# Scores and values of a gated linear attention by halves of keys, without the square above the diagonal

## The chip, the cores and the metric

The kernel runs on one core of a Trainium2 chip. The metric is the device time of one execution in microseconds (us). The kernel before took 387.55 us, the median of three runs (387.32 to 389.53).

A core has five engines that run their own instruction streams and wait for each other through semaphores: TensorE (PE in the profile, with its weight loads apart as PEld), VectorE (DVE), ScalarE (ACT), GpSimd (POOL) and SyncE (SP, which here issues most transfers). TensorE multiplies a stationary operand, loaded first, with a moving operand, and writes its result to PSUM. Its array can be split by rows and columns into tiles that work side by side; a matmul's `tile_position` names its tile.

## The reference

Four batches, eight heads, 768 tokens, 48 values a head: a recurrent state, then a two-layer block with a softmax-like unit and a norm.

```python
for t in range(S):
    state = alpha[:, :, t, :, None] * state + np.einsum('bhd,bhe->bhde', k[:, :, t], v[:, :, t])
    y[:, :, t] = np.einsum('bhd,bhde->bhe', q[:, :, t], state)
x = y.transpose(0, 2, 1, 3).reshape(B * S, H * D)      # 3072 x 384
h = x @ w_in                                           # 384 x 1024
sm = softmax(h); solu = h * sm
ln = (solu - mean(solu)) / np.sqrt(var(solu) + 1e-06) * g_ln
out = ln @ w_out                                       # 1024 x 384
```

Everything is float32.

## The kernel before, in words

**Groups.** The 768 tokens are cut into six groups of 128 (`G`), each for all four batches. For one group the attention part is done for all batches and heads at once. The 48 values of a head are split into 32 "firsts" and 16 "lasts", and the lasts of two heads share one block of 32. So q and k lie as (batch, 32 values) on the 128 partitions, token in the free dimension: `kT[quarter(b), block]`, `qv[quarter(b), block]`. Scans on VectorE (`scan_back`, `scan_on`) make the decays within a group, and q and k are multiplied with them, so that a plain product of q and k has the decay in it.

**Attention of a group**, in the order of its steps:

- `scores(g, half)`: four heads of all four batches. For each head two matmuls of 32 rows of contraction (firsts, then lasts) give a square of 128 keys on the partitions by 128 queries in the free dimension. The four batches use the four row tiles. Each batch has a PSUM bank of its own (`a0` to `a3`).
- `masked(half)`: VectorE multiplies each bank with an upper triangular mask of 128 columns (a query reads keys up to itself) and writes `sT` in SBUF; one operation of 512 columns a bank.
- `read_begin`, `read_state(half)`: from group 1 on, the old state times q, into PSUM banks `y` (they are the same four banks). Here the contraction is 64 rows, two batches at once, and the output is split in four column tiles: eight tiles.
- `read_values(g)`: 16 pieces (`parts`) of 32 output columns a batch, with the 128 keys as rows: `vn` (the values, token on the partitions, each head in 64 columns) is stationary, `sT` moves. Four column tiles. It goes batch by batch, and ScalarE copies each batch's bank to `x` when that batch is done.
- `next_state(g)`: products of `kg` (k with token on the partitions) and `vn` in two banks `kv`, which are `a0` and `a1` again, and an add to the state on VectorE.

**The block after it.** For each group `up` makes `h` in eight steps of 512 columns (L390), ScalarE the exp (L404), VectorE h times exp (L405), ScalarE its square (L406), and POOL and VectorE running sums (`running`, L421). `down` (L501) multiplies with `w_out`, in two halves for each of the group's four batches; `finish` scales and stores.

**What sets the order.** It is written by hand: each engine executes its instructions in program order. From group 1 on a loop runs over steps 0 to 7 of `up` of group g. In each step stand `up`, half a `down` of the group before it, and what a table names for the attention of group g+1: in the table `usual` `"v keys"` at step 0, the lasts and firsts of q at 2, `scores0` at the end of step 4, `masked0` at the head of 5, `scores1` at the end of 5, `masked1` at the head of 6, `read0` at 6, `read1` in 7, and `values` (with `next_state`) at the end of 7. In `first`, for the attention of group 2, there is no `down` yet. The attention of groups 0 and 1 is written out before the loop, with the unpacking of the weights: `fetch` brings them as 64-bit values into `room`, `bits` turns them to float32 on VectorE, and `in_range` tests their exponents on ScalarE, with a buffer `sq` in between.

**Queues.** `load_v(g)` puts four transfers on SP's queue. Behind it on the same queue come the loads of k, the moves of q to the rows of the state (`move_lasts`, `move_firsts`), the loads of q and alpha, and the stores of the output.

Of the kernel before, what the change touches and what calls it, by code (L numbers as in the profile page):

```python
# [32 lines left out]
def fast_path(ctx, tc, q, k, v, alpha, moe_w_in, moe_w_out, moe_g_ln, out):  # L33
# [12 lines left out]
    nc = tc.nc  # L46
    B, H, S, D = q.shape
    NTOK, DM = out.shape
# [3 lines left out]
    NP = H // 2  # L52
    NB = H + NP
    E0, E1 = 32, 16
    KC = DM // P
# [9 lines left out]
    const = pool("const", 1)  # L65
    ring = pool("ring", 3)
    work = pool("work", 2)
# [7 lines left out]
    ctx.enter_context(tc.manual_schedule())  # L75

    ident = const.tile([P, P], FP, name="ident")
    mask = const.tile([P, P], FP, name="mask")
    ones = const.tile([P, P], FP, name="ones")
    small_ones = const.tile([P, 32], FP, name="small_ones")  # L80
    parity = const.tile([P, 2], FP, name="parity")
# [23 lines left out]
    HW = 64  # L105
    VW = H * HW + E1
    vn = const.tile([P, B, VW], FP, name="vn")
    state = const.tile([P, 2, VW], FP, name="state")
    SW = P + 1
    lot = const.tile([P, 4 * 768], FP, name="lot")  # L110
# [58 lines left out]
    def held(x, n):  # L169

        return x[:, n, 0 : H * HW].rearrange("p (h e) -> p h e", e=HW)[:, :, E1:HW]

    def load_v(g):
        t = slice(g * P, (g + 1) * P)
        for b in range(B):
            nc.sync.dma_start(out=held(vn, b), in_=v[b, :, t, :].rearrange("h p d -> p h d"))

    def firsts(src, dst):
        nc.vector.transpose(out=dst.rearrange("p h (t u) -> p h u t", u=TQ), in_=src[:, :, :, 0:E0])  # L179
# [11 lines left out]

    def alpha_over(g):
        x = an.rearrange("p h u d -> p (h u d)")
        sq = one.tile([P, 768], FP, name="sq").bitcast(U8)[:, 0 : x.shape[1]]
# [73 lines left out]
    def quarter(b):  # L268
        return slice(32 * b, 32 * b + 32)

    def banks(name, shape, n=B):
        return [ps_a.tile([P] + shape, FP, tag=f"a{b}", name=f"{name}{b}") for b in range(n)]

    def scores(g, half, a=None):
        a = a or banks("a", [NP, P])
        for i in range(NP):
            h = half * NP + i
            for kb, qb in ((h, h), (H + h // 2, H + h)):
                for b in range(B):
                    nc.tensor.matmul(  # L280
                        a[b][:, i], lhsT=kT[quarter(b), kb], rhs=qv[quarter(b), qb, 0:P], start=kb == h, stop=kb != h,
                        tile_position=(32 * b, 0), skip_group_check=True,
                    )
        masks[half] = a

    masks = {}

    def masked(half, batches=range(B)):
        a = masks[half]
        for b in batches:  # L290
            nc.vector.tensor_tensor(  # L291
                out=sT[:, b, half * NP : half * NP + NP], in0=a[b], in1=mask[:, None, :].to_broadcast([P, NP, P]),
                op=ALU.mult,
            )

    def keys_back(g, t=None):
        t = t or banks("tp", [NP, P], 3)
# [25 lines left out]
    parts += [(3 * j + 1, 2 * j + 1, last) for j in range(NP)]  # L323
    reading = {}

    def y_mm(b, n, row, lhsT, rhs, stop=False):
        begun = reading["begun"]
        a, r = divmod(n, 4)
        nc.tensor.matmul(  # L329
            y_bank(b)[quarter(r), a], lhsT=lhsT, rhs=rhs, start=(b, r) not in begun, stop=stop,  # L330
            tile_position=(row, 32 * r), skip_group_check=True,
        )
        begun.add((b, r))
# [5 lines left out]
    def y_bank(b):  # L339
        if b not in reading["y"]:  # L340
            reading["y"][b] = ps_a.tile([P, KC, P], FP, tag=f"a{b}", name=f"y{b}")
        return reading["y"][b]
# [9 lines left out]
    def read_values(g, batches=range(B)):  # L352
        if 0 in batches:
            gr[g]["x"] = pair.tile([P, KC, B, P], FP, name="x")
# [93 lines left out]
    def token_sums(g):  # L448


        d = gr[g]
        t = ps_a.tile([P, B, 2, 32], FP, tag="a3", name="rows") if g else ps_h.tile([P, B, 2, 32], FP, tag="h", name="rows")
        for b in range(B):
            for r in range(4):
                c = b * P + 32 * r
                nc.tensor.matmul(
                    t[quarter(r), b], lhsT=d["unit"][:, 0:32], rhs=d["p"][:, :, c : c + 32], start=True, stop=True,
                    tile_position=(0, 32 * r), skip_group_check=True,
                )
        tt = work.tile([P, B, 2, 32], FP, name="cols")  # L460
# [45 lines left out]
    def finish(n):  # L506
        g, b = divmod(n, B)
        d = st[n]
        s, o = sums[:, n], d["o"][:, 0:DM]
        t0 = b * S + g * P  # L510
        if g == G - 1:
            o_sb = work.tile([P, DM], FP, name="o_sb")
            r = gr[g]["r"][:, b : b + 1]
            nc.vector.tensor_scalar(out=o_sb[:, 0:P], in0=o[:, 0:P], scalar1=r, scalar2=None, op0=ALU.mult)  # L514
            nc.scalar.activation(out=o_sb[:, P:DM], in_=o[:, P:DM], func=AF.Copy, scale=r)  # L515
            nc.scalar.dma_start(out=out[t0 : t0 + P, :], in_=o_sb)
            d.clear()
            return
        nc.vector.tensor_copy(out=s[:, 0:1], in_=d["o"][:, DM : DM + 1])
        t = small.tile([P, 1], FP, name="t")  # L520
        nc.vector.scalar_tensor_tensor(
            out=t, in0=s[:, 0:1], scalar=-1.0 / DFF, in1=s[:, 0:1], op0=ALU.mult, op1=ALU.mult
        )
        nc.vector.tensor_tensor(out=s[:, 3:4], in0=t, in1=gr[g]["s"][:, b : b + 1], op=ALU.add)  # L524
        if g == 0:

            o = work.tile([P, DM], FP, name="o_mean")
# [91 lines left out]
    def mean(half):  # L619


        m = ps_h.tile([P, 512], FP, tag="h", name="sums")[:, 0:DM]
        if half == 0:
            for f in range(FC):
                r = quarter(f % 4)
                nc.tensor.matmul(
                    m[r], lhsT=ones[:, 0:32], rhs=w_out[:, f, 0:DM], start=f < 4, stop=f >= FC - 4,
                    tile_position=(0, r.start), skip_group_check=True,
                )
            made["m"] = work.tile([P, DM], FP, name="o_mean")  # L630
# [14 lines left out]
    nc.scalar.dma_start(out=mask, in_=inline(np.triu(np.ones((P, P))), "mask_c"))  # L645
# [764 lines left out]
```

## Time and profile before

| | |
|---|---|
| median of three runs | 387.55 us |
| the profiled execution: time, span | 388.88 us, 387.1 us |
| TensorE busy, records | 365.6 us (94%), 4341 matmuls and 4341 weight loads |
| VectorE, ScalarE, GpSimd busy | 250.7, 144.5, 111.5 us |
| `h` (L390), `o` (L501) on PE | 134.8, 133.1 us |
| scores in banks `a` (L280) on PE | 26.2 us, 704 records |
| values, and reads of the state (L329), on PE | 22.6 us, 768 records; 11.9 us, 640 records |
| mask (L291) on VectorE | 27.3 us, 44 of 683 ns, and 4 in other banks |
| copies of `x` (L359) on ScalarE | 11.2 us, 24 of 480 ns |
| mean granted TensorE clock | 0.989 |

The span is the time from the first to the last instruction of one profiled execution. A float32 matmul leaves two matmul records and two weight-load records. The busy time of a line counts overlapping records once, so 704 records of 289 ns make 26.2 us, since four tiles work side by side. "Idle before" is how long the engine stood still just ahead of a group of instructions, with what ended it. "issue" is a stall that ended with nothing that the profile shows as released. "PEclk" is the share of TensorE's full clock that was granted.

### The profile page before, as it was taken

To read this page: it belongs to the slowest core of one execution; us is meant where nothing else is said; L and a number is where in the kernel's file an instruction comes from. 1 tells how busy PE (TensorE), PEld (TensorE's weight loads), DVE (VectorE), ACT (ScalarE), POOL (GpSimd) and SP (SyncE) were. 2 spreads that over 40 slices of the span, in tenths; PEclk is the share of its full clock that TensorE was granted. 3 is DMA by queue.
4 is the path that set the end of the run, shared out by engine and by line. 5 is a ranking of instruction groups with operands and counts; after the bars stand their busy time and mean duration, and the time that the engine had idled before them with its cause. 6 is when DMAs were issued, how large, how long until landed. Compare 5 with 4: busy or idle time off the path is not lost. (4 is left out here: it accounts for less than half of the span.)

```text
span 387.1 us, 10060 instructions
## 1 busy us (share of the span) xinstructions
PE 365.6 (94%) x4341; PEld 219.3 (57%) x4341; DVE 250.7 (65%) x413; ACT 144.5 (37%) x255; POOL 111.5 (29%) x122
## 2 busy tenths in 40 slices
PE   8798899988979998999999999998999999999994
PEld 8685335656645556555557555665556565555652
DVE  0989878996997858885584875664875413444600
ACT  2628566681415426134253153342142132222100
POOL 6000000000232992437130466210475211323200
PEclk9989999999989999999999999999999999999999
DMA  9891978248355535717142627003123000000011
GB/s 182 166 323 51 221 220 200 47 97 183 92 131 104 116 79 102 147 35 161 37 105 47 140 62 172 13 11 70 36 63 89 22 16 8 23 21 20 22 44 47
DMA packets 72439, 36.05 MB, mean 93 GB/s; under 512 B 48185, under 2 KB 69953, under 8 KB 72385
## 3 DMA queue, kind: packets, MB, share of 16 engines
q1 hardware_dynamic: 71360, 34.39, 37.6%
q10 hardware_dynamic: 1024, 0.92, 0.7%
q8 instruction: 36, 0.59, 0.7%
q14 instruction: 19, 0.15, 0.1%
HBM read 25.30 MB, written 4.72 MB: 78 GB/s over the span
## 5 line engine op out<-in xcount | busy, mean ns | idle before, releaser
L390 PE MATMUL h<-x,w_in 128*128 128x512 f32 x288 | 134.8, 608 | 3.4 <-DVE room L405 1.6
L501 PE MATMUL o<-w_out,room 128*128 128x385 f32 x384 | 133.1, 491 | 1.1 <-DVE least L218 1.1
L501 PEld LDWEIGHTS o<-w_out,room 128*128 128x128 f32 x384 | 71.6, 190 | 56.8 <-issue 15.3
L390 PEld LDWEIGHTS h<-x,w_in 128*128 128x128 f32 x288 | 53.1, 192 | 63.5 <-issue 49.2
L405 DVE TENSOR_TENSOR room<-h,e 128x512 f32<-128x512 f32 x40 | 27.7, 693 | 62.6 <-ACT e L404 62.6
L404 ACT ACTIVATE e<-h 128x512 f32<-128x512 f32 x40 | 23.9, 597 | 89.1 <-PE h L390 88.5
L421 POOL TENSOR_TENSOR p<-p,e 128x512 f32<-128x512 f32 x30 | 40.8, 1360 | 21.9 <-ACT e L404 21.5
L406 ACT ACTIVATE u<-room 128x512 f32<-128x512 f32 x40 | 25.2, 630 | 42.5 <-DVE room L405 42.5
L532 POOL TENSOR_TENSOR r<-sums,mhalf 128x1 f32<-128x1 f32 x20 | 12.5, 626 | 91.5 <-DVE sums L524 91.5
L291 DVE TENSOR_TENSOR sT<-a,mask 128x512 f32<-128x512 f32 x44 | 27.3, 683 | 15.3 <-PE a L280 15.3
L280 PE MATMUL a<-qv,kT 32*128 32x128 f32 x704 | 26.2, 289 | 3.9 <-DVE least L218 2.0
L280 PEld LDWEIGHTS a<-qv,kT 32*128 32x128 f32 x704 | 23.2, 196 | 11.0 <-issue 2.3
L421 DVE TENSOR_TENSOR p<-p,u 128x512 f32<-128x512 f32 x30 | 23.6, 786 | 8.4 <-ACT u L406 8.4
L204 DVE TENSOR_TENSOR_SCAN hT<-aT,unit 128x516 f32<-128x516 f32 x18 | 22.3, 1285 | 8.7 <-ACT aT L677 8.6
L204 DVE TENSOR_TENSOR_SCAN aT<-aT,seed 128x516 f32<-128x516 f32 x18 | 25.0, 1391 | 0.6
L329 PE MATMUL y<-sT,vn 128*32 128x128 f32 x768 | 22.6, 273 | 0.4 <-DVE sT L291 0.4
L329 PEld LDWEIGHTS y<-sT,vn 128*32 128x32 f32 x768 | 20.7, 110 | 2.9 <-issue 2.0
L228 POOL TENSOR_TENSOR kT<-kT,hT 128x1024 f32<-128x1024 f32 (+1 forms) x8 | 13.3, 1682 | 29.8 <-DVE kT L179 29.8
L359 ACT COPY x<-y 128x384 f32<-128x384 f32 x24 | 11.2, 480 | 22.7 <-PE y L329 22.7
L196 ACT ACTIVATE sq<-an,mone 128x1536 uint8<-128x1536 f32 x12 | 18.9, 1572 | 0.2
L243 POOL COPY qe<-hT 128x4 f32<-128x4 f32 x5 | 1.0, 191 | 59.4 <-DVE hT L204 59.4
L534 ACT ACTIVATE o_sb<-o,r 128x384 f32<-128x384 f32 x16 | 9.3, 581 | 17.2 <-POOL r L532 17.2
(142 smaller groups left out, 370.2 us busy)
## 6 DMA issues: line engine op xcount, KB each, us to landing
vn<-in_v_dram SPq DMA_DIRECT2D x24, 192.0 KB, 4.5
an<-in_alpha_dram SPq DMA_DIRECT2D x20, 192.0 KB, 4.1
out_dram<-o_sb SPq DMA_DIRECT2D x20, 192.0 KB, 2.0
room<-in_moe_w_in_dram SPq DMA_DIRECT2D x6, 512.0 KB, 7.5
room<-in_moe_w_out_dram SPq DMA_DIRECT2D x8, 384.0 KB, 4.3
kn<-in_k_dram SPq DMA_DIRECT2D x16, 192.0 KB, 3.9
qn<-in_q_dram SPq DMA_DIRECT2D x16, 192.0 KB, 4.7
lot<-qe SPq DMA_DIRECT2D x40, 64.5 KB, 2.1
```

The costliest lines, as they stand in the source:

```text
L196: nc.scalar.activation(out=sq, in_=x, func=AF.Relu, scale=sign, bias=mone, accum_out=over[:, g, i : i + 1])
L204: nc.vector.tensor_tensor_scan(out=o, data0=a, data1=s, initial=1.0, op0=ALU.mult, op1=ALU.add)
L228: nc.gpsimd.tensor_tensor(out=kT[:, part], in0=kT[:, part], in1=hk[:, part], op=ALU.mult)
L280: nc.tensor.matmul(a[b][:, i], lhsT=kT[quarter(b), kb], rhs=qv[quarter(b), qb, 0:P], start=kb == h, stop=kb != h, tile_position=(32 * b, 0 ...
L291: nc.vector.tensor_tensor(out=sT[:, b, half * NP : half * NP + NP], in0=a[b], in1=mask[:, None, :].to_broadcast([P, NP, P]), op=ALU.mult,)
L329: nc.tensor.matmul(y_bank(b)[quarter(r), a], lhsT=lhsT, rhs=rhs, start=(b, r) not in begun, stop=stop, tile_position=(row, 32 * r), skip_g ...
L390: nc.tensor.matmul(h, lhsT=w_in[:, a, f * P : (f + 1) * P], rhs=d["x"][:, a].rearrange("p b t -> p (b t)"), start=(a == 0), stop=(a == KC ...
L404: nc.scalar.activation(out=e, in_=h, func=AF.Exp)
L405: nc.vector.tensor_tensor(out=u, in0=h, in1=e, op=ALU.mult)
L406: nc.scalar.activation(out=u2, in_=u, func=AF.Square)
L421: eng.tensor_tensor(out=p, in0=d[0][i] if f == 1 else p, in1=d[f][i], op=ALU.add)
L501: nc.tensor.matmul(d["o"][:, 0 : DM + 1], lhsT=u_of(g, f)[:, b * P : b * P + P], rhs=w_out[:, f], start=(f == 0), stop=(f == FC - 1), skip ...
```

## The change

Scores and values are both cut in halves of 64 keys, and the square of 64 keys by 64 queries in which every query lies before every key is left out.

**Scores.** A score matmul becomes two, with 64 keys each, in two column tiles: eight tiles (32 rows by 64 columns). The half with the later keys multiplies only the later 64 queries. The lasts of a pair of heads are done in one matmul of two blocks of queries. From group 1 on, in every second pair of heads the halves are exchanged (`swapped`): the later keys go to partitions 0 to 63. A bank then has in its columns 0 to 63 the squares on the diagonal, and in its columns 64 to 127, on one half of the partitions, the square of early keys and late queries.

**Mask and copy.** VectorE multiplies columns 0 to 63 alone with a mask of 64 columns. The square in columns 64 to 127 needs no mask, and ScalarE copies it: two copies of 64 partitions by 128 columns a bank from group 1 on, one of 256 columns in group 0.

**Values.** They are read by halves of keys, in eight tiles of 64 rows by 32 columns, with 128 or 64 queries. [...]there are two turns: batches c and c+2, with one half of the keys each, and then the other halves. Between the turns ScalarE copies one column of the bank (`seen`), which the next turn waits for. The exchanged pairs need their values with the halves exchanged too: `vw`, which eight further transfers a group fill from `vn`.

**Room.** To make place for `vw`, `sq` is 384 wide, `in_range` works in place on `room`, and `cols` and `o_mean` have one buffer for two.

```diff
-    mask = const.tile([P, P], FP, name="mask")
+    HP = P // 2
+    mask = const.tile([P, HP], FP, name="mask")
...
+        for b in range(B) if g else ():
+            x = vn[:, b, 0 : H * HW].rearrange("p (j i e) -> p j i e", i=2, e=2 * HW)[:, :, 1]
+            for r in range(2):
+                nc.sync.dma_start(out=vw[HP * r : HP * r + HP, b], in_=x[HP - HP * r : P - HP * r])
...
+    def swapped(g, j):
+
+        return j % 2 if g else 0
+
     def scores(g, half, a=None):
         a = a or banks("a", [NP, P])
-        for i in range(NP):
-            h = half * NP + i
-            for kb, qb in ((h, h), (H + h // 2, H + h)):
+        p, n = 2 * half, half * NP
+        blocks = [(n + 2 * j + i, n + 2 * j + i, 1) for i in range(2) for j in range(2)]
+        blocks += [(H + p + j, H + n + 2 * j, 2) for j in range(2)]
+        for x, (kb, qb, m) in enumerate(blocks):
+            i = qb - n - (H if m == 2 else 0)
+            for r in range(2):
+                s = HP * (r ^ swapped(g, i // 2))
                 for b in range(B):
                     nc.tensor.matmul(
-                        a[b][:, i], lhsT=kT[quarter(b), kb], rhs=qv[quarter(b), qb, 0:P], start=kb == h, stop=kb != h,
-                        tile_position=(32 * b, 0), skip_group_check=True,
+                        a[b][HP * r : HP * r + HP, i : i + m, 0 : P - s], lhsT=kT[quarter(b), kb, s : s + HP],
+                        rhs=qv[quarter(b), qb : qb + m, s:P], start=x == 0, stop=m == 2,
+                        tile_position=(32 * b, HP * r), skip_group_check=True,
                     )
...
-            nc.vector.tensor_tensor(
-                out=sT[:, b, half * NP : half * NP + NP], in0=a[b], in1=mask[:, None, :].to_broadcast([P, NP, P]),
-                op=ALU.mult,
-            )
+            nc.vector.tensor_tensor(
+                out=out[:, :, 0:HP], in0=a[b][:, :, 0:HP], in1=mask[:, None, :].to_broadcast([P, NP, HP]), op=ALU.mult
+            )
+            for p, i in (
+                ((slice(0, HP), slice(0, 2)), (slice(HP, P), slice(2, 4))) if g else ((slice(0, HP), slice(0, NP)),)
+            ):
+                nc.scalar.copy(out=out[p, i, HP:P], in_=a[b][p, i, HP:P])
...
-        for b in batches:
-            for m, (n, h, e) in enumerate(parts):
-                y_mm(b, n, 0, vn[:, b, e(h)], sT[:, b, h], m >= len(parts) - 4)
-        for b in batches:
-            nc.scalar.copy(out=gr[g]["x"][:, :, b], in_=reading["y"][b])
+        for turn in range(2):
+            for c in range(2):
+                for n, h, e in parts[::-1] if turn else parts:
+                    j = h // 2
+                    for r in range(2):
+                        b = 2 * (r ^ turn) + c
+                        p = slice(HP * r, HP * r + HP)
+                        at = HP * (r ^ swapped(g, j))
+                        if swapped(g, j):
+                            cols = e(h)
+                            lhsT = vw[p, b, j // 2, cols.start - 2 * HW * j : cols.stop - 2 * HW * j]
+                        else:
+                            lhsT = vn[p, b, e(h)]
+                        y_mm(b, n, HP * r, lhsT, sT[p, b, h, 0 : P - at], turn == 1 and n < 4, at)
+                x = reading["y"]
+                if turn == 0:
+                    n = parts[-1][0]
+                    seen = small.tile([P, 1], FP, name="seen")
+                    nc.scalar.copy(out=seen[quarter(n % 4)], in_=x[b][quarter(n % 4), n // 4, P - 1 : P])
+                else:
+                    for b in (c, c + 2):
+                        nc.scalar.copy(out=gr[g]["x"][:, :, b], in_=x[b])
...
-        sq = one.tile([P, F], FP, name="sq").rearrange("p (c f) -> p c f", c=hi.shape[1])
-        nc.scalar.activation(out=sq, in_=hi, func=AF.Square, accum_out=far[:, i, 0:1])
-        nc.scalar.activation(out=sq, in_=sq, func=AF.Exp, scale=-(2.0**24), accum_out=far[:, i, 1:2])
+        nc.scalar.activation(out=hi, in_=hi, func=AF.Square, accum_out=far[:, i, 0:1])
+        nc.scalar.activation(out=hi, in_=hi, func=AF.Exp, scale=-(2.0**24), accum_out=far[:, i, 1:2])
```

More of the change, by code (lines that the diff above doesn't have):

```diff
@@ L107, in fast_path @@
     vn = const.tile([P, B, VW], FP, name="vn")
+    vw = const.tile([P, B, NP // 2, 2 * HW], FP, name="vw")
     state = const.tile([P, 2, VW], FP, name="state")
@@ L193, in alpha_over @@
         x = an.rearrange("p h u d -> p (h u d)")
-        sq = one.tile([P, 768], FP, name="sq").bitcast(U8)[:, 0 : x.shape[1]]
+        sq = one.tile([P, 384], FP, name="sq").bitcast(U8)[:, 0 : x.shape[1]]
         for i, sign in enumerate((1.0, -1.0)):
@@ L272, in banks @@
         return [ps_a.tile([P] + shape, FP, tag=f"a{b}", name=f"{name}{b}") for b in range(n)]
+    def swapped(g, j):
+        return j % 2 if g else 0
     def scores(g, half, a=None):
         a = a or banks("a", [NP, P])
-        for i in range(NP):
-            h = half * NP + i
-            for kb, qb in ((h, h), (H + h // 2, H + h)):
+        p, n = 2 * half, half * NP
[5 more added lines that the diff above has]
+                s = HP * (r ^ swapped(g, i // 2))
                 for b in range(B):
                     nc.tensor.matmul(
-                        a[b][:, i], lhsT=kT[quarter(b), kb], rhs=qv[quarter(b), qb, 0:P], start=kb == h, stop=kb != h,
-                        tile_position=(32 * b, 0), skip_group_check=True,
+                        a[b][HP * r : HP * r + HP, i : i + m, 0 : P - s], lhsT=kT[quarter(b), kb, s : s + HP],
+                        rhs=qv[quarter(b), qb : qb + m, s:P], start=x == 0, stop=m == 2,
+                        tile_position=(32 * b, HP * r), skip_group_check=True,
                     )
-        masks[half] = a
+        masks[half] = g, a
     masks = {}
     def masked(half, batches=range(B)):
-        a = masks[half]
+        g, a = masks[half]
         for b in batches:
+            out = sT[:, b, half * NP : half * NP + NP]
             nc.vector.tensor_tensor(
-                out=sT[:, b, half * NP : half * NP + NP], in0=a[b], in1=mask[:, None, :].to_broadcast([P, NP, P]),
-                op=ALU.mult,
-            )
+                out=out[:, :, 0:HP], in0=a[b][:, :, 0:HP], in1=mask[:, None, :].to_broadcast([P, NP, HP]), op=ALU.mult
+            )
+            for p, i in (
+                ((slice(0, HP), slice(0, 2)), (slice(HP, P), slice(2, 4))) if g else ((slice(0, HP), slice(0, NP)),)
+            ):
+                nc.scalar.copy(out=out[p, i, HP:P], in_=a[b][p, i, HP:P])
     def keys_back(g, t=None):
@@ L324, in fast_path, with y_mm @@
     reading = {}
-    def y_mm(b, n, row, lhsT, rhs, stop=False):
+    def y_mm(b, n, row, lhsT, rhs, stop=False, at=0):
         begun = reading["begun"]
@@ L329, in y_mm @@
         nc.tensor.matmul(
-            y_bank(b)[quarter(r), a], lhsT=lhsT, rhs=rhs, start=(b, r) not in begun, stop=stop,
+            y_bank(b)[quarter(r), a, at:P], lhsT=lhsT, rhs=rhs, start=(b, r) not in begun, stop=stop,
             tile_position=(row, 32 * r), skip_group_check=True,
@@ L350, in read_state, with read_values @@
                         y_mm(2 * i + c, n, 64 * i, state[p, c, e(h)], q64[p, c, h, 0:P])
-    def read_values(g, batches=range(B)):
-        if 0 in batches:
-            gr[g]["x"] = pair.tile([P, KC, B, P], FP, name="x")
-        for b in batches:
-            for m, (n, h, e) in enumerate(parts):
-                y_mm(b, n, 0, vn[:, b, e(h)], sT[:, b, h], m >= len(parts) - 4)
-        for b in batches:
-            nc.scalar.copy(out=gr[g]["x"][:, :, b], in_=reading["y"][b])
+    def read_values(g):
+        gr[g]["x"] = pair.tile([P, KC, B, P], FP, name="x")
+        for turn in range(2):
[20 more added lines that the diff above has]
+                        nc.scalar.copy(out=gr[g]["x"][:, :, b], in_=x[b])
     def next_state(g):
@@ L459, in token_sums @@
                 )
-        tt = work.tile([P, B, 2, 32], FP, name="cols")
+        tt = one.tile([P, B, 2, 32], FP, name="cols")
         nc.vector.transpose(out=tt.rearrange("p b i t -> p (b i t)"), in_=t.rearrange("p b i t -> p (b i t)"))
@@ L525, in finish @@
         if g == 0:
-            o = work.tile([P, DM], FP, name="o_mean")
+            o = one.tile([P, DM], FP, name="o_mean")
             nc.vector.scalar_tensor_tensor(
@@ L629, in mean @@
                 )
-            made["m"] = work.tile([P, DM], FP, name="o_mean")
+            made["m"] = one.tile([P, DM], FP, name="o_mean")
             nc.scalar.mul(out=made["m"], in_=m, mul=-1.0 / (32 * DFF))
@@ L644, in fast_path @@
     nc.scalar.dma_start(out=ident, in_=inline(np.eye(P), "ident_c"))
-    nc.scalar.dma_start(out=mask, in_=inline(np.triu(np.ones((P, P))), "mask_c"))
+    nc.scalar.dma_start(out=mask, in_=inline(np.tile(np.triu(np.ones((HP, HP))), (2, 1)), "mask_c"))
     odd = np.arange(P) // E1 % 2
```

## The prediction

> **What bounds the kernel now.** First the page: TensorE (PE) is busy 94% of the span. Second, the time line of PE in one steady group (151 to 207 us), where its bursts follow each other without idle time.
>
> ```profile
> PE 365.6 (94%) x4341; PEld 219.3 (57%) x4341; DVE 250.7 (65%) x413; ACT 144.5 (37%) x255; POOL 111.5 (29%) x122
> ...
> q8 instruction: 36, 0.59, 0.7%
> ```
> ```profile
> 179.49 2.07 PE L280 MATMUL a<-qv,kT 32*128 32x128 f32 x64
> 181.48 2.84 PE L390 MATMUL h<-x,w_in 128*128 128x512 f32 x6
> ...
> 194.21 1.17 PE L329 MATMUL y<-lot,state 64*32 64x128 f32 x64
> 195.31 2.84 PE L390 MATMUL h<-x,w_in 128*128 128x512 f32 x6
> ...
> 201.96 3.70 PE L329 MATMUL y<-sT,vn 128*32 128x128 f32 x128
> 205.47 1.54 PE L367 MATMUL kv<-vn,kg 128*32 128x48 f32 x128
> 206.95 2.84 PE L390 MATMUL h<-x,w_in 128*128 128x512 f32 x6
> ```
> Columns: start, length, engine and line, tiles, records. Start to start, a half of the scores costs 1.99 us (181.48-179.49), half a state read 1.10, the values 3.51, the kv products 1.48. So in steady state PE time is kernel time. Third, the stalls that PE does have, and the counts of PE instructions between them:
>
> ```profile
> 13.77 0.31 PE L164 MATMUL tp_k<-ident,lot 128*32 128x128 f32 x3 [0.49 <-issue]
> ```
> ```profile
> 107.70 1.46 PE L367 MATMUL kv<-vn,kg 128*32 128x48 f32 x120
> 111.65 0.29 PE L367 MATMUL kv<-vn,kg 128*32 128x48 f32 x8 [2.49 <-issue]
> ...
> 261.15 1.45 PE L367 MATMUL kv<-vn,kg 128*32 128x48 f32 x118
> 263.84 0.36 PE L367 MATMUL kv<-vn,kg 128*32 128x48 f32 x10 [1.23 <-issue]
> ```
> ```profile
> 13.40:111.60 98.20, 86.44 (x1400) 54.14 (x1400) 86.25 (x128) 51.96 (x99) 7.00 (x11) 0.98 0.63 157
> 111.60:263.80 152.20, 149.19 (x1906) 88.32 (x1906) 105.96 (x160) 57.01 (x98) 63.57 (x66) 0.99 0.39 88
> ```
> The second columns of the windows are PE and weight-load records. 1400+1400 and PE's 16 semaphore records are 2816 = 11 x 256; 1906+1906+28 are 3840 = 15 x 256. All three "issue" stalls stand at a multiple of 256 PE instructions, and the page's instruction queue moved 36 packets, 0.59 MB, 16 KB each. PE waited for its program.
>
> [...]
>
> **The time of one block.** The block that ran out at 108.95 began at 107.39 (240 instructions of kv and the last 16 or so of the values) and its successor came at 111.65: 4.3 us later. The other: 260.8 to 263.84, 3.0 us; the first: 9.4 to 13.77, 4.4 us. A block of 202.5 to 205.7 (3.2 us) had no gap. [...] I take 4.0 in groups 3 to 5, and 4.2 in groups 1 and 2, where transfers are denser (the DMA engines' busy share is 0.42 in 100 to 112 and 0.50 in 145 to 155, 0.02 in 257 to 266); ends 3.5 and 4.8. [...]it can then run one block of 256 per such time, however short the block's own work.
>
> **Scores.** Per half 32 matmuls on 4 tiles become 48 on 8 (32x64). Columns per tile: 128+64+128+64+256+128 = 768, from 8x128 = 1024; records 16 to 12. [...]1.99 to 1.55. No row shows 32x64 tiles; bounds: 1.55, and 1.99 if issue of more records eats it. I take -0.44, ten times (groups 1 to 5): -4.4. Group 0 has no exchange: one row of tiles keeps 1024 columns, 0. Each half has 192 PE instructions for 128, with some 5 us of thin work (12 of h, 16 of o) after it: under one block per 4 us, no stall.
>
> **Values.** 64 matmuls become 128; PE instructions (a matmul is four) 256 to 512. [...]2.64 us for 3.51, if the program arrives. The state read, 8 tiles of 64x32 too, ran 64 records in 1.10 us[...]. Two further hand-offs: turn 1 waits for the "seen" copy (0.28 us after the quarter's last issue, as for x, and 0.2 us of copy: hidden by the 0.66 us of the other quarter); and kv's second bank needs x of batch 1, now made after the last matmul: 0.28, the rest of batch 2's copy and 0.48 of its own, some 1.0 us where kv waited for nothing. Alone that would eat the 0.87 gain.
>
> But values and kv are now 768 instructions, three blocks, that ask for 4.2 us of work. Counting PE instructions in program order (transposes two, waits one), boundaries continue every 256 from those in the trace:
> - group 1: 110th of the second state read; 238th and 494th of values; 238th of kv. [...]end 12.0 us for 7.69 (104.18 to 111.87): +4.3.
> - group 2: 104th, then 232, 488, kv 232: 12.0 for 6.54: +5.5.
> - group 3: 32, 288, kv 32: the first block is requested in the o ahead and arrives in time; 1.2+4.0 at kv 32, then 1.2: 6.4 for 4.99: +1.4.
> - group 4: 88, 344, kv 88: 0.1+8.0+0.9 = 9.0 for 6.49: +2.5.
> - group 5: 171, 427, no kv: 0.56+4.0+0.4, then 1.3 for the last two x copies: 6.3 for 4.30: +2.0.
> Sum +15.7; with 3.5 us +10, with 4.6 to 4.8 +19.
>
> **Group 0.** Boundaries at the 55th and 311th of the scores' 384 instructions and the 182nd and 438th of values. Transfers fill 20 to 28 us, and the values end some 1.9 us (block 3.9) to 5.7 us (block 4.5 to 5.5) after their 29.55. Then ScalarE's row of x, kg, and the range test of the weights, which ran without a gap from 29.68 to the first exp at 35.87, moves with it, and VectorE's chain behind that exp (L405, bits) holds PE until 89.5. +4.0, bounds +2 and +6. The in-place range test waits for the second of bits' operations alone, done before: 0.
>
> **The rest.** VectorE's mask is 256 columns for 512: 683 ns to about 0.42; 48 of them save VectorE 13 us, but it is not what PE waits for: 0. ScalarE gets 88 copies, each after the mask of its bank. By L306 (391 ns for 256) and L301 (579 for 512) 128 columns are 0.3 us, 4.8 us a group; ScalarE waits 4.41 and 5.38 us for h before its exps at 184.42 and 191.78, which hides them: 0, and if that cover were gone, 1 to 2 us a group. SP issues eight more copies of 64 KB after each load of v, each once v has landed (4.5 us): some 10 us of queue, idle in the usual groups. In group 2 the moves of q follow close (125.92) and come 1 to 2 us later; POOL's decay and the state read behind them: +0.5, bounds 0 and +1.5. Smaller buffers from one pool: their next writer comes 5 us or more after the reader, 0.
>
> **Sum.** -4.4+15.7+4.0+0.5 = +15.8 on the profiled execution's 388.88 us: 404.7. That run lies 1.3 us above the median, so 403.
>
> **Rivals.** (1) The blocks arrive in time, and PE's shorter work is the time: -4.4 and, with x copied in time, 5x0.7: 380 to 383, say 382. For it: two of five kv bursts stalled, not all; against it: the stalls stand on multiples of 256. It decides if a block needs under 1.4 us. (2) The program arrives, but the hand-offs x to kv, seen, and decay eat the gain: -4.4+0.5+0.5 to 2: 385 to 388, no difference. For it: kv already once waited 1.04 us for x; against: it needs the fetch hidden too. (3) Besides the stalls the clock falls: after the 2.49 us stall the granted clock was 0.57 in 112 to 116; one such window a group costs up to 1.7 us, so up to 411. [...]
>
> **Chances.** Fetch-bound 0.83 (of it 0.12 with a fallen clock), rival 2 0.08, rival 1 0.09. Range of the first: 388.9-1.3-4.4 with 10+2 and with 19+6+1.5: 394 to 410; one fallen clock or two more, and a block of 3.3 us: 392 to 412, which leaves out the other two cases and little else. One per cent is about what can be told from no change: faster 0.09, same 0.07, slower 0.84.
>
> **What would show it.** Right: idle PE in L348 and the kv line put down to "issue", 1.5 to 3 us at multiples of 256 instructions; over 44 instruction packets; values 4.7 to 7 us; scores bursts near 1.55 us start to start; first exp of the weights stage after 37.5 us. Wrong: values in 2.7 us with no issue idle, or the waits of kv named ScalarE's x.

## The result, and the profile after

The kernel after takes 409.82 us (median of four, 405.94 to 412.39), the kernel before 388.36 us (median of four): 1.053 times as long, 95% interval 1.046 to 1.060. The ratio leaves out the longest execution of after, 412.39 us, which at 1.6% above the shortest counts as slow; it is the one that was profiled, 2.6 us above the median. Its mean clock is 0.972, that of the shortest, 405.94 us, is 0.989, as before: the clock is part of the difference, below.

The page of after, PE and the instruction queue:

```profile
PE 373.9 (91%) x5493; PEld 219.1 (53%) x5493; DVE 239.8 (58%) x413; ACT 169.2 (41%) x355; POOL 112.1 (27%) x122
...
q8 instruction: 45, 0.74, 0.8%
```

PE is busier by 8 us and yet a smaller share of the span, so it also waits more. The instruction queue moved 45 packets for 36: nine more of 256 instructions each, for 2304 more PE instructions (1152 more matmul records, each with a weight load). Nothing else grew into a bound: VectorE lost 11 us, ScalarE gained 25 us and is at 41%.

The time line of PE for one steady group's scores, as shown of before (start, length, engine and line, tiles, records):

```profile
194.71 1.86 PE L294 MATMUL a<-qv,kT 32*64 32x128 f32 x96
196.50 2.84 PE L426 MATMUL h<-x,w_in 128*128 128x512 f32 x6
```

Start to start 1.79 us, for 1.99 before. Now the values and kv of group 1, then of group 2; shown are the rows with idle time ahead (in brackets, with what ended it), and the first rows behind:

```profile
112.32 0.30 PE L348 MATMUL y<-sT,vw 64*32 64x64 f32 x2 [1.83 <-issue]
...
116.87 0.43 PE L348 MATMUL y<-sT,vn 64*32 64x128 f32 x11 [2.51 <-issue]
117.22 0.29 PE L403 MATMUL kv<-vn,kg 128*32 128x48 f32 x8
117.90 2.44 PE L403 MATMUL kv<-vn,kg 128*32 128x48 f32 x109 [0.38 <-ACT x L395]
120.87 0.53 PE L403 MATMUL kv<-vn,kg 128*32 128x48 f32 x11 [0.53 <-issue]
121.33 1.12 PE L426 MATMUL h<-x,w_in 128*128 128x512 f32 x2
...
157.63 0.30 PE L348 MATMUL y<-sT,vw 64*32 64x64 f32 x2 [1.15 <-ACT seen L392]
...
160.03 0.27 PE L348 MATMUL y<-sT,vw 64*32 64x128 f32 x1 [0.64 <-issue]
160.40 0.29 PE L403 MATMUL kv<-vn,kg 128*32 128x48 f32 x8
161.09 1.38 PE L403 MATMUL kv<-vn,kg 128*32 128x48 f32 x106 [0.40 <-ACT x L395]
164.58 0.37 PE L403 MATMUL kv<-vn,kg 128*32 128x48 f32 x14 [2.11 <-issue]
164.88 4.54 PE L426 MATMUL h<-x,w_in 128*128 128x512 f32 x6
```

Read the starts of the rows behind an "issue": 112.32, 116.87, 120.87 in group 1; 156.03 (not shown), 160.03, 164.58 in group 2. They are 4.55, 4.00, 4.00 and 4.55 us apart: that is how fast blocks of program came here, whatever PE had to do between. Counted in PE instructions as in the prediction, all eleven stalls of this trace that are put to "issue" stand whole multiples of 256 apart, to within one record. The last row shows what follows: six records of `h` take 4.54 us for 2.84.

The trace also has the packets of the instruction queue (q8) one by one. Those of group 1 end at 111.05, 115.36 and 119.55 us, and PE goes on at 112.32, 116.87 and 120.87. In this trace each of the eleven stalls ends 1.25 to 1.57 us after such a packet has ended, and the 93 such stalls of 0.25 us or more in the fourteen traces of this case end 1.15 to 1.67 us after one. A block's time can be read from the same rows: PE goes on at 112.32, the next packet begins 1.79 us later and takes 1.25 us, and PE goes on 1.51 us after its end, 4.55 us in all.

The clock around these places, windows of the trace (window, its length, busy us and records of PE, PEld, DVE, ACT, POOL, granted PE clock, DMA share, GB/s):

```profile
117.80:121.40 3.60, 2.97 (x121) 2.68 (x121) 1.02 (x2) 0.43 (x2) 0.00 (x0) 0.53 0.13 24
...
164.88:169.40 4.52, 4.52 (x15) 1.54 (x13) 1.02 (x2) 0.00 (x0) 0.00 (x0) 0.62 0.60 118
169.40:172.00 2.60, 2.60 (x40) 1.70 (x40) 1.74 (x6) 1.23 (x2) 0.00 (x0) 1.00 0.85 178
```

Behind these stalls PE runs at half its clock. The trace's record of the granted clock has 0.50 for 6.83 us from 25.79, and for 3.41 us each from 117.95, 165.74, 281.79 and 339.81; behind the stall of 0.71 us in group 3 there is none. The kernel before has two such windows of 3.41 us, from 20.16 and 112.32. (Both traces also have one in their last microseconds.)

**Where the 23.5 us between the two spans lie**, from start times in both time lines:

| stretch | before | after | difference |
|---|---|---|---|
| start to the scores of group 1 | 87.73 | 92.62 | +4.9 |
| values to the next h, group 1 | 7.69 | 12.62 | +4.9 |
| group 2 | 6.54 | 11.99 | +5.5 |
| group 3 | 4.99 | 6.72 | +1.7 |
| group 4 | 6.49 | 9.60 | +3.1 |
| group 5 | 4.30 | 6.16 | +1.9 |
| all else (387.1 and 410.6 less the above) | 269.4 | 270.9 | +1.5 |

The values with kv take 17.1 us of it, the start 4.9 us. "All else" holds the saving of the scores and the cost of the fallen clock in `h`, which nearly cancel. The rows of `h` behind the values, from their start to the next row, differ by -1.7 us in group 1 (there the kernel before had its own window), +1.7, +0.8 and +1.7 us in groups 2, 4 and 5: 2.5 us, and the page's `h` on PE grew from 134.8 to 137.2 us. The rest of the fallen windows lies within the start and kv.

### The profile page after: what moved, and what is told of

It reads as the page before. It is cut to its first block, busy times and chain, and to the rows that moved or that the text cites. A ratio compares the mean times of both kernels' runs of the same rounds, so it can differ in the third digit from the quotient of the medians.

```text
span 410.6 us, 12540 instructions
## 1 busy us (share of the span) xinstructions
PE 373.9 (91%) x5493; PEld 219.1 (53%) x5493; DVE 239.8 (58%) x413; ACT 169.2 (41%) x355; POOL 112.1 (27%) x122
## 3 DMA queue, kind: packets, MB, share of 16 engines
q10 hardware_dynamic: 1024, 0.89, 0.6%
## 5 line engine op out<-in xcount | busy, mean ns | idle before, releaser
L426 PE MATMUL h<-x,w_in 128*128 128x512 f32 x288 | 137.2, 616 | 3.7 <-DVE room L441 2.7
L537 PEld LDWEIGHTS o<-w_out,room 128*128 128x128 f32 x384 | 71.5, 190 | 57.1 <-issue 15.7
L313 ACT COPY sT<-a 64x128 f32<-64x128 f32 (+1 forms) x84 | 22.2, 265 | 21.4 <-DVE sT L307 20.2
L348 PE MATMUL y<-sT,vn 64*32 64x128 f32 (+1 forms) x896 | 27.1, 269 | 4.0 <-issue 3.9
L348 PEld LDWEIGHTS y<-sT,vn 64*32 64x32 f32 x896 | 22.8, 113 | 7.6 <-issue 7.1
L294 PE MATMUL a<-qv,kT 32*64 32x128 f32 (+2 forms) x1056 | 22.4, 280 | 4.1 <-DVE least L224 1.7
L348 PE MATMUL y<-sT,vw 64*32 64x128 f32 (+1 forms) x640 | 19.2, 249 | 5.8 <-issue 4.7
L294 PEld LDWEIGHTS a<-qv,kT 32*64 32x64 f32 x1056 | 17.6, 130 | 11.6 <-POOL p L457 2.2
L307 DVE TENSOR_TENSOR sT<-a,mask 128x256 f32<-128x256 f32 x44 | 15.5, 414 | 13.4 <-PE a L294 13.4
L202 ACT ACTIVATE sq<-an,mone 128x1536 uint8<-128x1536 f32 x12 | 18.9, 1572 | 0.2
```

The source lines that it names most:

```text
L202: nc.scalar.activation(out=sq, in_=x, func=AF.Relu, scale=sign, bias=mone, accum_out=over[:, g, i : i + 1])
L294: nc.tensor.matmul(a[b][HP * r : HP * r + HP, i : i + m, 0 : P - s], lhsT=kT[quarter(b), kb, s : s + HP], rhs=qv[quarter(b), qb : qb + m, ...
L307: nc.vector.tensor_tensor(out=out[:, :, 0:HP], in0=a[b][:, :, 0:HP], in1=mask[:, None, :].to_broadcast([P, NP, HP]), op=ALU.mult)
L313: nc.scalar.copy(out=out[p, i, HP:P], in_=a[b][p, i, HP:P])
L348: nc.tensor.matmul(y_bank(b)[quarter(r), a, at:P], lhsT=lhsT, rhs=rhs, start=(b, r) not in begun, stop=stop, tile_position=(row, 32 * r), ...
L426: nc.tensor.matmul(h, lhsT=w_in[:, a, f * P : (f + 1) * P], rhs=d["x"][:, a].rearrange("p b t -> p (b t)"), start=(a == 0), stop=(a == KC ...
```

## The experiments

Times stand against runs of the kernel before on the same chip: 387.80 us in the first set of four, 387.37 in the second, 388.01 in the third and 387.81 beside the last run. A time against the kernel after is a comparison of medians from different sets.

### More instructions alone

The kernel before, each value matmul cut in two:

```diff
-                y_mm(b, n, 0, vn[:, b, e(h)], sT[:, b, h], m >= len(parts) - 4)
+                for i in range(2):
+                    cols = slice(64 * i, 64 * i + 64)
+                    y_mm(b, n, 0, vn[:, b, e(h)], sT[:, b, h, cols], i == 1 and m >= len(parts) - 4, cols)
```

> The kernel before, with each of its 64 value matmuls of 128 queries cut in two of 64: the same columns, the same four tiles and waits, no turns, no copies by ScalarE, but 512 PE instructions for 256 in each group's values. Theory (PE waits for blocks of 256 instructions): values and kv are again three blocks in a row, so idle PE put to issue at L329 and at kv, values start to the next h 6 to 12 us a group for 4.3 to 7.7, 398 to 407 us in all against some 388 before. Rival (the new time lies in the turns, the seen copies, the copies of x behind the last matmul or the two row tiles): values 3.6 us, 388 to 391 us in all.

406.55 us, 1.046 (1.042 to 1.051) of before. Nothing of the change is in this kernel but the larger number of value instructions, and a cost of 18.8 us is there. Its waits of PE (us in total, times, longest), and group 1 in its time line:

```profile
PE y L329 <- issue: 11.1, 8, 1.8
PE kv L369 <- issue: 8.5, 4, 3.7
```
```profile
106.03 2.09 PE L329 MATMUL y<-sT,vn 128*32 128x64 f32 x120
109.46 2.15 PE L329 MATMUL y<-sT,vn 128*32 128x64 f32 x128 [1.34 <-issue]
113.19 0.26 PE L329 MATMUL y<-sT,vn 128*32 128x64 f32 x2 [1.57 <-issue]
...
118.56 0.39 PE L369 MATMUL kv<-vn,kg 128*32 128x48 f32 x8 [3.67 <-issue]
118.88 2.93 PE L392 MATMUL h<-x,w_in 128*128 128x512 f32 x3
```

128 matmul records between two stalls are 256 instructions with their weight loads. Values to h are 12.85 us in group 1 (7.69 before). Stalls put to issue make 19.6 us in these two lines, for 3.7 before, so most of the cost is stall. A part is work: 128 records here take 1.94 us from the first start to the last, so I estimate 3.9 us for 256, for 3.43 before. The turns, the copies `seen`, the copies of `x` and the row tiles are not needed to explain a slowdown of this size.

### Group 0 undone

The kernel after with the scores, mask and values of group 0 as in the kernel before (`if g == 0:` in three functions, and a second mask).

> The kernel after, with scores, mask and values of group 0 as before (a mask of 128 columns beside the one of 64), all else of the change kept, the range test in place too. Theory (group 0's 512 instructions of values and 384 of scores are late): first exp of the weights stage back near 35.9 us, scores of group 1 begin near 89.5 to 90.5 instead of 92.6, total 3 to 6 us under the kernel after. Rival (the start is late through the range test in place or the smaller buffers): no more than 1.5 us gained.

405.98 us, 3.8 us under the median of after, which is in the expected range; but the two sets of four overlap (404.66 to 408.33 and 405.94 to 412.39), so the start times say more than the total. Its first exp of the weights stage starts at 35.10 us (after 41.09, before 35.87), the scores of group 1 at 86.68 (after 92.62, before 87.73), with the range test still in place. The late start comes with group 0's extra instructions. In the kernel after, PE's longest stall for the program stands in group 0's scores, and its values run at half clock (0.50 from 25.79 to 32.62 us); the run with group 0 undone has no window of half clock before 114 us:

```profile
25.87 0.36 PE L294 MATMUL a_h<-qv,kT 32*64 32x64 f32 x1 [3.32 <-issue]
27.81 6.97 PE L348 MATMUL y<-sT,vn 64*32 64x128 f32 x256
41.09 0.57 ACT L440 ACTIVATE sT<-h 128x512 f32<-128x512 f32 x1
```
```profile
35.10 0.57 ACT L464 ACTIVATE sT<-h 128x512 f32<-128x512 f32 x1
```

The first fence is of the kernel after, the second of this run.

Group 0 now has 384 PE instructions less, so all later multiples of 256 move by half a block. In group 3 this run has:

```profile
216.26 0.24 PE L365 MATMUL y<-sT,vn 64*32 64x64 f32 x1 [1.48 <-issue]
...
217.79 0.97 PE L427 MATMUL kv<-vn,kg 128*32 128x48 f32 x70 [0.36 <-ACT x L419]
219.71 0.78 PE L427 MATMUL kv<-vn,kg 128*32 128x48 f32 x50 [0.95 <-issue]
```

where the kernel after had run its values through, and had one small stall in kv:

```profile
216.89 0.32 PE L348 MATMUL y<-sT,vn 64*32 64x128 f32 x6
...
220.59 0.29 PE L403 MATMUL kv<-vn,kg 128*32 128x48 f32 x8
221.25 0.29 PE L403 MATMUL kv<-vn,kg 128*32 128x48 f32 x6 [0.36 <-ACT x L395]
222.24 1.44 PE L403 MATMUL kv<-vn,kg 128*32 128x48 f32 x114 [0.71 <-issue]
```

Values to h are 8.78 us for 6.72 there, in the same work; in group 5 it is 4.77 for 6.16. The stalls go with the place in the program, not with what is computed. The time of a block is no constant: the two stalls of group 3 above stand 3.45 us apart, those of group 1 in this run 5.65 (108.84 and 114.49).

### Scores alone

The run above, with `read_values` of before for all groups and without the transfers of `vw`.

> Scores, mask and ScalarE's copies by halves from group 1 on, values as before over all 128 keys, no exchanged values and their transfers, group 0 as before. The output is not the reference's: the values are not exchanged and read the left-out square as it was left. Theory: a half of the scores takes 1.79 us for 1.99, ten times, and the values stay one block: 385.5 to 388 us, issue stalls as few as before. Rival (the copies behind the mask hold the values up, or the scores' 192 instructions stall too): 389 us or more, with idle PE ahead of the values put to ScalarE.

387.27 us, 0.9985 (0.9968 to 1.0002): as expected, no difference that can be told. (One of its 20 executions took 869.62 us; it is not in the ratio, and its cause is not known.) A half of the scores is 1.80 us. PE's waits for the program in kv are about those of before (3.7 us there):

```profile
PE kv L427 <- issue: 3.2, 3, 1.9
```

So scores of 192 instructions a half do not stall in groups 1 to 5, and the mask and ScalarE's copies hold nothing up that shows. Ten halves at 0.2 us make some 2 us of PE's time; the total shows 0.5 us less, of an interval from 1.2 us less to 0.1 more.

### Half of the values

```diff
-                for n, h, e in parts[::-1] if turn else parts:
+                for m, (n, h, e) in enumerate(parts[::-1] if turn else parts):
+                    if g and m % 8 // 4 == turn:
+                        continue
```

> The kernel after, with half of the value matmuls of groups 1 to 5 left out (so x is not the reference's): 256 PE instructions for 512, the turns, the seen copies, the copies of x and the transfers kept. The work left out is 1.8 us a group, 9 us. Theory: with it go some 11 us of issue stalls and most of the windows of the fallen clock, 384 to 391 us in all (the late start stays). Rival (hand-offs make the time): no more than the 9 us, 397 to 402 us.

393.79 us, 16 us under the kernel after: more than the 9 us of work left out, and less than expected. Issue stalls in values and kv fell to 3.7 and 2.0 us (8.6 and 4.8 in after). What I had missed stands in group 2:

```profile
156.61 0.42 PE L348 MATMUL y<-sT,vw 64*32 64x64 f32 x2 [3.58 <-ACT seen L394]
```

ScalarE did its two tests of alpha (L202, two of 1.57 us) before it came to `seen`. In the kernel after the same wait is there (1.15 us at 157.63), in the shade of the blocks of program.

### Equal lengths side by side

The values ran at 27.5 ns a matmul where nothing stalled, not at the predicted 20.6 (2.64 us for 128; by columns alone, three quarters of the 3.51 us before, I estimate as much, with the work spread evenly over eight tiles). The kernel after, in another order (in groups 1 to 5 for the scores):

```diff
+            order += [(two[0], 0), (two[1], 1), (two[0], 1), (two[1], 0)] if g else [(x, r) for x in two for r in range(2)]
...
-                for n, h, e in parts[::-1] if turn else parts:
+                for (n, h, e), r, end in even[turn]:
```

> The kernel after, with the matmuls of scores and values in another order alone: in each round over the eight tiles all have the same number of queries (all 128, then all 64), where the kernel after puts a matmul of 64 queries beside one of 128 each time. The trace of after has values at 27.5 ns a matmul where nothing stalls (256 records from 216.89 in 3.52 us)[...] and a half of the scores at 1.79 us. Theory (instructions start in order, so the tile with 64 waits for its neighbour with 128): 20.6 to 22 ns a matmul in stretches without stall, a half of the scores 1.55 us, but behind three blocks of program the values to h gain only some 0.3 us a group: 2 to 5 us under the kernel after. Rival (a floor of 27 ns for issue or weight loads): stretches and scores as in after, no change in all.

411.73 us, as slow as after; a half of the scores 1.80 us, and 27.3 ns a matmul of the values in group 3. My theory fell: the order of lengths is not what keeps the matmuls from the predicted pace. The profiled execution here took 408.77 us, and in group 1 it stalls at the same three places of the program as after (113.35, 117.35 and 121.63 us).

### Few queries

In the kernel after, from group 1 on, value matmuls of 32 queries: `sT[p, b, h, 0 : (32 if g else P - at)]`.

> The kernel after, where from group 1 on each value matmul moves 32 queries only, for 128 or 64 (so x is not the reference's): the same number of instructions, a third of the columns. [...] Theory (a matmul of four instructions on these tiles has a floor by itself, which the run of equal lengths pointed to): stretches without stall at 22 to 27 ns a matmul, as with the full columns. Rival (columns, the longer of the neighbours): 15 ns or less. In both the blocks of program set the time of values and kv: the total within 2 per cent of the kernel after.

414.56 us (median of two), within 2% of after, though two thirds of the columns are gone: values and kv there wait for the program. The pace in stretches without stall is 17.6 to 19 ns a matmul, 2.6 to 2.8 times what columns alone would give (6.9 ns, an estimate from the kernel before: 54.8 ns a matmul of 128 queries on four tiles, 3.51 us for 64; a quarter of the columns, twice the tiles) and below the 22 to 27 I had expected. So columns don't explain the pace of these tiles; whatever limits it at 32 queries lies below the 26 to 28 ns of the full values. What sets those stays open.

### Thin work between the bursts

The order of the kernel after changed from group 1 on: state read, down, turn 0, up, down, turn 1, half a down of the next set (`early`), the next up, kv.

```diff
-        tail={4: "scores0", 5: "scores1", 6: "begin read0", 7: "values"},
-        middle={7: "read1"},
+        tail={4: "scores0", 5: "scores1", 6: "turn0", 7: "turn1 rest"},
+        middle={6: "begin read0 read1"},
...
+            if s == 0 and att:
+                next_state(g)
```

> The kernel after, with thin work put between its dense bursts from group 1 on: both halves of the state read before the down of step 6, turn 0 of the values behind it, up of step 7, its down, turn 1, one half of a down of the next set (of which only the first four u are needed), the next group's first up, and kv behind that. The same instructions, each 256 of the values and kv apart by 16 to 28 instructions of some 2.8 us. Theory (PE waits for its program): the issue stalls of groups 1 to 5 (some 13 us in the trace of after), the wait for x and the windows of the fallen clock go, the late start of 5 us stays: 387 to 394 us. Rival (the time is in the turns and hand-offs, or PE's gaps come by number of instructions in all): 400 us or more.

411.48 us: no gain, so the expectation failed, and the total lies where the rival had it. But the waits of PE are other ones:

```profile
PE h L426 <- ACT x L395: 9.7, 4, 3.2
PE y L348 <- issue: 4.7, 3, 2.1
```

and the time lines of PE (first row) and ScalarE in group 3 show why x was late:

```profile
223.42 4.54 PE L426 MATMUL h<-x,w_in 128*128 128x512 f32 x6 [3.24 <-ACT x L395]
...
218.50 1.56 ACT L202 ACTIVATE sq<-an,mone 128x1536 uint8<-128x1536 f32 x1
...
220.19 1.57 ACT L202 ACTIVATE sq<-an,mone 128x1536 uint8<-128x1536 f32 x1
...
221.76 1.60 ACT L395 COPY x<-y 128x384 f32<-128x384 f32 x4
```

With the steps I had moved the alpha test in front of the copies of x. The run with both edits and group 0 as before had the same fault:

> Both, with group 0 as in the kernel before. Theory: against the kernel before ten halves of scores at -0.44, five values at -0.8, its own issue stalls of 3 to 4 us less: 375 to 382 us. Rival (order of equal lengths gives nothing): 382 to 387 us.

401.61 us, beyond both ranges, with 10.0 us of waits for x; it tells nothing on the order of lengths. Both again, with the alpha test a step earlier (`6: "alpha", 7: "back"`):

> The order of the thin run, with ScalarE's alpha test (L202, two of 1.57 us) back at step 6, ahead of turn 0, where the thin run had moved it to step 7, in front of the copies of x. Theory: the thin run's 9.7 us of waits of h for ScalarE's x (four of up to 3.2) were my own edit, and each let the clock fall for some 3.4 us; with them gone 13 to 20 us less than the thin run: 391 to 398 us, with the late start of 5 us and no issue stall over 1.5 us from group 2 on. Rival (the copies of x hold h up by themselves): waits of h for x of 1 us or more in each group, 400 us or more.

402.17 us, 9.3 us under the first try and 4 us over the expectation. The total lies where the rival had it, but the waits of h for x are down to 2.5 us, three of at most 1.0. In groups 3 to 5 no stall is left in values or kv; groups 1 and 2 still have some of up to 1.8 us, and there are 2.0 us at a step I had not thought of (`rows`, 64 instructions behind kv's 256).

> The same repair to the run with both edits and group 0 as before. Theory: 10.0 us of waits for x and three to four windows of the fallen clock less than its 401.6 us: 383 to 388 us, beside 387.4 for the kernel before and 385.2 for that kernel with its kv moved. Rival: waits for x stay, 394 us or more.

391.43 us; again some 3 us over. ScalarE in group 4:

```profile
265.11 0.58 ACT L624 ACTIVATE o_sb<-o,r 128x384 f32<-128x384 f32 x1 [1.31 <-POOL r L622]
265.58 1.61 ACT L449 COPY x<-y 128x384 f32<-128x384 f32 x4
```

The output `o_sb`, which `finish` makes at step 7, waited for GpSimd, with x behind it. The last run moves this `finish` behind turn 1:

```diff
-            if after is not None:
+            if after is not None and (s < FC - 1 or not att):
...
                 if what == "rest":
+                    if after is not None:
+                        finish(after)
+                        after = None
```

> The run before this one in that line (thin, equal lengths, group 0 as before, the alpha test at step 6), with the finish of step 7 moved behind turn 1: in that run's trace of group 4 ScalarE's o_sb waited 1.31 us for POOL's r at 265.11, and the four copies of x stood behind it, so that h waited 0.87 us for x. Theory (the last hand-off of the change that is on the path from group 3 on): some 1 us a group in two to three groups, 2 to 4 us less than its 391.4 us: 387 to 390 us, no better than the kernel before. Rival (x is late by its own four copies): h waits for x as long as it did, no change.

387.94 us, 1.0009 (0.9991 to 1.0028) of before: as expected. Some stalls are left:

```profile
PE y L372 <- issue: 2.5, 3, 1.2
```

With group 0 restored and most stalls and hand-offs out of the way, the change from group 1 on gains nothing over the plain kernel before.

### The same thinning for the kernel before

In the part written out before the loop, `down(3, 1)` moves behind the values of group 1; in the loop:

```diff
             at("tail", s)
+            if s == FC - 1 and att:
+                down(*early)
...
+            if s == 0 and att:
+                next_state(g)
```

> The kernel before, with half a down between its values and the next up, and kv behind that up: values and kv no longer two blocks in a row. Theory: its stalls of 2.49 and 1.23 us in kv, the fallen clock of 112 to 116 (some 1.9 us) and the waits of kv for x (1.0 us) go: 382 to 385 us. Rival (x is waited for by the up instead): 387 to 389 us.

385.23 us, 0.9943 (0.9923 to 0.9964): 0.2 us beyond the expected stretch, and the fastest kernel of all here. kv has no issue stall left (3.7 us before), and no wait for x:

```profile
PE h L390 <- DVE room L405: 4.1, 4, 2.4
...
PE y L329 <- issue: 0.6, 2, 0.3
```

The first line was 1.6 us before: a wait of 2.41 us for VectorE in group 1 is new, with a window of half clock at 115.53 us, so this order is not free of cost either. With the program thinned in both kernels, the one with the change is 2.7 us slower (387.94 and 385.23 us, medians of different sets).

## Why the prediction was right

Slower was right, and so was the reason; 403 us was 6.8 us under the median of after, inside the range of 392 to 412. Little luck was in it: between the spans 23.5 us were measured for +15.8, and the larger terms all missed to the same side. Of the signs named, 45 packets, the stalls and the late first exp came; a half of the scores near 1.55 us did not. Step by step:

- **The bound.** Blocks of program of 256 instructions held PE, at the multiples counted: shown by the added instructions alone (+18.8 us), by the stalls that moved with group 0's program, and by the packets of the instruction queue that end just ahead of each stall's end. The blocks came late for 768 instructions in 4 to 5 us of work (13.4 us of stalls in values and kv of after), and for the scores of group 0 (a stall of 3.32 us); in the scores of groups 1 to 5 after has no stall put to "issue".
- **The time of one block.** 4.0 and 4.2 us taken, with ends of 3.5 and 4.8. In after it is 4.00 or 4.55 in groups 1 and 2 and 4.00 in group 4; over all traces two stalls one block apart stand 3.45 to 5.65 us apart, so the ends were too narrow. How long before its need a block is asked for, which the sums by group take in, was my estimate; no run shows it.
- **Values and kv.** Predicted 12.0, 12.0, 6.4, 9.0 and 6.3 us to the next h, measured 12.62, 11.99, 6.72, 9.60 and 6.16: +17.1 for +15.7.
- **Values if the program arrived.** Mis-sized: 2.64 us predicted, 3.70 measured in group 3, no faster than the 3.51 before. What it cost behind the blocks was not separated; but with it, and with the scores as below, rival 1 could not have given 382.
- **Scores.** The term that failed most: -0.44 a half, -4.4 in all; measured -0.20 and -2.0. The 1.55 us was my estimate. 768 columns per tile for 1024, three quarters, took 1.79 us for 1.99, nine tenths; what set this stays open (equal lengths: 1.80 us).
- **Group 0.** +4.0 predicted, +4.9 measured, by the way named: x, kg and the range test late, first exp at 41.09 for 35.87. A part is the fallen clock, 6.83 us at half for 3.41 before.
- **The seen copy.** That the other quarter hides it was wrong in group 2, where ScalarE was in the alpha test; 1.15 us, itself covered by the wait for the next block. The prediction did not count what ScalarE has queued ahead of it. What the turns are needed for is not shown: no run here has the values by halves without them.
- **x to kv.** 0.4 us of wait a group for 1.0 predicted, and 0.99 ahead of h in group 5.
- **The decay in group 2.** Its first state read takes 1.71 us for 1.09: +0.6 for +0.5.
- **Mask and copies.** 414 ns for 420 and 265 ns for 300, hidden, by the run of the scores alone. The range test in place: the early start of the run with group 0 undone leaves it nothing to explain.
- **The clock.** Rival 3, to which I had given 0.12, came about: the sum had nothing for the clock, the range one or two windows. The windows at half clock stand behind the stalls of groups 1, 2, 4 and 5 and at the start. Of the spans' 23.5 us, -2.0, +17.1, +4.9 and +0.6 make 20.6; of the other 2.9 us the rows of `h` show 2.5. What the clock adds within kv and the start, no run separates.

The last kernel's 387.94 us lies in the 385 to 388 of rival 2, but this does not confirm its sum: that kernel has another order, and its stalls for the program are 2.9 us, where before had 4.2.

## What to carry to other kernels

Count instructions, not only columns: before cutting matmuls into smaller ones, count the engine's instructions in each burst, mark the multiples of a block (256 in these traces) from the stalls that the trace already has, and give each block the time that two such stalls in a row show (3.5 to 5.7 us in these traces). Where a burst has more, put long instructions of other work between its parts (the kernel before then had no stall in kv, for 3.7 us), and read what every engine has to do ahead of the hand-offs that this moves (9.7 us of waits for x in the first try). And when a stall is cured, look at the plain kernel with the same cure: here it gained 0.6% (0.9943 of before), and the change with it nothing (1.0009).

## What the runs showed that was not expected

- 128 matmuls of 96 queries on average, on eight tiles of 64 rows by 32 columns, take about as long as 64 of 128 queries on four tiles of 128 by 32 (3.70 and 3.51 us to the next work in group 3): 27.5 ns each, 27.3 with equal lengths side by side, 17.6 to 19 with 32 queries. With other work between the turns it is 26.7 to 27.2 ns, and 26.3 with equal lengths too. By columns alone, from the 54.8 ns of a matmul of 128 queries on the four tiles of before, I estimate 20.6 and 6.9 ns. What takes the rest is not shown.
- One wait of 3.24 us of PE cost some 1.7 us more: behind it six records of `h` take 4.54 us for 2.84 (the thin run, 223.42 us; the clock is 0.50 for 3.41 us from 224.25). A single wait for ScalarE thus does what a stall for the program does. The clock also fell behind one of 2.11 us (164.58 us in the kernel after), and in group 4 behind two of 1.11 and 1.43 us, four us apart.
